# Retention attention in f32 products without halves, inside an attention and two-MoE kernel

## The chip, the cores and the metric

The kernel runs on one core of one Trainium2 chip. The metric is the time of one execution on the device in microseconds; the time of a kernel is the median of its runs. A core has five engines that this text names as the profile does: PE multiplies matrices (PEld is its loading of weights), DVE is the vector engine, ACT the scalar engine, POOL is GpSimd, SP issues most of the transfers. Sixteen DMA engines carry the transfers.

## What is computed

The input is q, k, v of 8 sequences, 8 heads, 576 positions and 64 dimensions. First comes a retention attention (scores with a decay in place of a softmax), then two mixture-of-experts layers on 4608 rows of 512, in which each row goes to one of 8 experts:

```python
scores = scale * np.matmul(q, k.transpose(0, 1, 3, 2))
gamma = 1.0 - 2.0 ** (-5.0 - np.arange(H, dtype=np.float32))
Dmat = np.where(rel >= 0, gamma[:, None, None] ** rel[None, :, :], 0.0)   # rel = i - j
ret = scores * Dmat[None, :, :, :]
return np.matmul(ret, v).astype(np.float32)
...
x = _moe_ref(x=x, **moe_kwargs)        # argmax expert, relu(x @ w1) @ w2, two gates
return _moe2_ref(x=x, **moe2_kwargs)   # the same with a bias by modality and one gate
```

The change touches the attention alone. The routing needs the attention to nearly f32 accuracy, since an argmax that falls otherwise sends a row to another expert.

## The kernel before

The program has two parts. `attention_and_routing` makes the attention output of each tile, its logits and its expert, and scatters the rows into the DRAM buffer `xs1`, sorted by expert. `experts` then runs the two layers from `xs1`; the change does not touch it.

The attention works on 36 chunks of 128 positions and all 8 heads: four per sequence (c = 0 to 3), and one for the last 64 positions of two sequences together (c = 4, the tail). A decay splits into a factor of the key's position, put on v (`v_scale`), and one of the query's position, put on the output (`out`), so the scores only need the causal mask. What earlier chunks of a sequence give comes through a state of 64 by 64 per head, which `kv` and `state` carry from chunk to chunk (`gC` is the decay over one chunk).

PE takes f16 here, so each f32 operand is held as two halves, hi and lo (`k_hi` and `k_lo`, `q_hi` and `q_lo`, `v_hi` and `v_lo`, `a_hi` and `a_lo`, `state_hi` and `state_lo`), and a product is three products, `PASSES = ((0, 0), (0, 1), (1, 0))`. ACT makes the hi halves, DVE and POOL the lo halves. Per chunk:

- three loads of 256 KB on SP's queue (L298): k and v by position, q already transposed in DRAM;
- `transposes` (L329): 8 PE transposes of the halves of k into PSUM, which ACT copies out (`kT_out`);
- `scores` (L350): 24 products, by pairs of heads; the two heads of a pair stand in partitions 0 to 63 and 64 to 127, use the two row halves of the array and write the tiles pa0 and pa1;
- heads of parity 0: DVE masks pa0 into f32 (`a_full`, L420), and `av_full` multiplies with v in f32, four products, the only f32 products of the attention; the trace records each as two matmuls and two weight loads;
- heads of parity 1: hi half by ACT, lo half by DVE (L279), both masked on POOL (L369), and 12 products in `av` (L404);
- `kv` (L377): 24 products and two that add the old state through an identity (L379); `state` (L383);
- `qS` (L404): 24 products of q with the state, in two calls;
- `out` (L431) on DVE, a row scale by `squares` and `row_scale` (L435 to L446), the two halves of the row (`x_hi` on ACT, `x_lo` on DVE, L453), a transposing DMA on SP's queue (L455), and 8 products for the logits (L462).

Groups of 4 or 5 chunks are routed by a chain of about 20 short DVE operations (`route`, L207 to L268), and POOL scatters their rows (L203). The eight first weight pieces of each matrix of expert 0 are converted at the end of this part (L547, L548).

Every engine works in program order. The order is a table, `PLAN`: each step has a beat (one beat is one chunk), given apart for the five kinds of chunk; all steps are sorted by beat. `FIRST` shifts the steps of the first five chunks, `GATES` places the loads and splits of the gate weights, `STEPS` the routing chain.

Of the kernel before, what the change touches and what calls it, by code (L numbers as in the profile page):

```python
# [30 lines left out]
QS, KS, VS = 32.0, 32.0, 16.0  # L31
# [4 lines left out]
    "k_hi": (-2.028, -2.770, -3.081, -2.909, -2.763),  # L36
    "vs": (-1.992, -2.348, -3.188, -1.669, -1.282),
    "k_lo": (-1.751, -2.064, -2.527, -2.579, -2.639),
    "q_hi": (-1.097, -1.702, -1.683, -2.485, -2.161),
    "pt": (-1.401, -1.677, -1.460, -1.290, -1.005),  # L40
    "v_hi": (-0.811, -1.371, -1.336, -0.862, -0.420),
    "q_lo": (-0.551, -1.252, -1.482, -1.253, -0.584),
    "v_lo": (-0.297, -1.046, -0.245, -0.372, 0.196),
    "kT": (-1.159, -0.874, -0.403, -0.701, -0.998),
    "S": (0.222, 0.181, 0.287, 0.260, 0.097),
    "am0": (0.334, 0.282, 0.531, 0.449, 0.187),
    "kv": (0.073, 0.524, 0.372, 0.505, 1.633),
    "Sn": (0.230, 0.575, 0.613, 0.695, 6.213),
    "ah1": (0.596, 0.631, 0.385, 0.518, 0.232),
    "qS0": (-13.770, 0.710, 0.694, 0.529, 0.219),  # L50
    "al1": (0.852, 0.937, 0.839, 0.769, 1.026),
    "Sh": (0.415, 0.944, 0.728, 0.797, -3.479),
    "av0": (0.922, 1.020, 1.097, 1.130, 1.208),
    "Sl": (0.564, 1.233, 0.996, 1.074, -2.260),
    "mh1": (1.231, 1.362, 1.017, 0.873, 1.420),
    "ml1": (1.412, 1.539, 1.052, 1.300, 1.605),
    "av1": (2.106, 1.795, 1.790, 1.802, 2.282),
    "qS1": (-8.214, 2.045, 1.567, 1.937, 1.514),
    "out": (2.400, 2.098, 1.999, 2.210, 2.465),
    "sq": (2.541, 2.150, 3.296, 2.949, 2.775),  # L60
    "rs1": (2.976, 2.479, 3.923, 3.559, 3.293),
    "rs2": (3.315, 3.092, 4.149, 3.806, 3.517),
    "xh": (3.754, 4.304, 4.598, 4.028, 3.781),
    "xl": (4.514, 5.247, 5.077, 4.665, 4.345),
    "lg": (6.437, 7.280, 6.703, 5.707, 5.721),
}
ENGINES = {"vs": "PPPPPPPPP", "v_lo": "PPPPPPPPP", "Sl": "PPPPPPPPP", "mh1": "PPPPPPPPP", "ml1": "PPPPPPPPD"}
FIRST = -3.462, -0.341, 0.344, 0.159, -0.039
GATES = -5.2, -1.440, -2.415, 1.091
WARM = 15  # L70
# [40 lines left out]
def attention_and_routing(tc, st, I, K):  # L111
# [173 lines left out]
    class Chunk:  # L285
# [54 lines left out]
        def q_lo(self):  # L340
            lo(self.qT[:, 1], self.qn, self.qT[:, 0], QS)
# [1141 lines left out]
```

## Time and profile before

| | us |
|---|---|
| median of 3 runs | 1131.69 (1131.39 to 1137.43) |
| the profiled execution | 1131.96 |
| its span, first to last instruction | 1130.2 |
| start until the first scores product | 12.3 |
| first scores product of chunk 0 to that of chunk 35 | 232.0 |
| from there to the first product of the experts | 44.3 |
| experts | 841.6 |

The page gives, over the whole span, PE busy 1025.8 us (91%), DVE 579.8 (51%), ACT 439.8 (39%), POOL 338.2 (30%), and a mean granted TensorE clock of 0.924. The experts hold three quarters of the span, so these shares tell little of the attention; it has to be read by itself. In the attention the row of the granted clock changes between 0.5 and 1.0, which are 1.2 and 2.4 GHz.

### The profile page before, as it was taken

Reading aid. Unit: us, or ns where it says so; the run is one execution under the profiler, and the core shown is the slowest. Engines: PE = TensorE matmul, PEld = TensorE weight load, DVE = VectorE, ACT = ScalarE, POOL = GpSimd, SP = SyncE. Lnnn points to the kernel's source line nnn. Section 1 sums busy time; section 2 is a strip of 40 time slices with the busy share of each in tenths; the row PEclk is TensorE's granted clock in tenths of the full one; section 3 lists DMA queues with packets and bytes.
Section 4 is the critical chain, followed back from the end, with each engine's and each line's share of the span. In section 5 each row is a group of like instructions: output and inputs, shape, how many; then the busy total and the mean of one; then the engine's idle time right before and its main releaser. Section 6 shows DMA issues by size and latency. Waiting matters only on the chain. (4 is left out here: it accounts for less than half of the span.)

```text
span 1130.2 us, 27289 instructions
## 1 busy us (share of the span) xinstructions
PE 1025.8 (91%) x10037; PEld 736.6 (65%) x10037; DVE 579.8 (51%) x1624; ACT 439.8 (39%) x833; POOL 338.2 (30%) x370
## 2 busy tenths in 40 slices
PE   8897788880799999999999999999999999999996
PEld 6786677770566767576666566667676667667664
DVE  7799999986455555555555565532412111111111
ACT  7767666743243434343434434323311111111111
POOL 7868788755112121212211121220110111011010
PEclk8858787865899999999999999999999999999999
DMA  8557677764666566657467455627211121221200
GB/s 297 136 146 188 189 199 199 176 198 126 228 187 149 143 147 151 139 141 144 141 174 172 78 159 128 150 61 208 67 48 45 48 67 40 54 50 47 56 28 31
DMA packets 213056, 145.07 MB, mean 128 GB/s; under 512 B 174089, under 2 KB 174253, under 8 KB 212912
## 3 DMA queue, kind: packets, MB, share of 16 engines
q1 hardware_dynamic: 203952, 114.63, 41.6%
q0 software_dynamic: 8960, 28.62, 7.2%
q8 instruction: 79, 1.29, 0.5%
q14 instruction: 65, 0.53, 0.2%
HBM read 70.75 MB, written 33.92 MB: 93 GB/s over the span
## 5 line engine op out<-in xcount | busy, mean ns | idle before, releaser
L1062 PE MATMUL ph<-xT,wb 128*128 128x256 f16 (+2 forms) x1344 | 338.7, 263 | 22.5 <-PEq L566 22.5
L1064 PE MATMUL ph<-xT,wb 128*128 128x256 f16 (+2 forms) x1344 | 338.8, 263 | 0.0
L1063 PE MATMUL ph<-xT,wb 128*128 128x256 f16 (+2 forms) x1344 | 338.7, 263 | 0.0
L1270 DVE SCALAR_TENSOR_TENSOR hT<-ph,hT 128x512 f16<-128x512 f32 (+2 forms) x168 | 106.5, 638 | 333.3 <-DVEq L566 332.4
L1070 PE MATMUL py<-wb,hT 128*128 128x512 f16 x608 | 231.0, 380 | 1.4 <-PEq L566 0.7
L1071 PE MATMUL py<-wb,hT 128*128 128x512 f16 x608 | 231.1, 380 | 0.0
L1072 PE MATMUL py<-wb,hT 128*128 128x512 f16 x608 | 230.9, 380 | 0.0
L1161 ACT ACTIVATE hT<-ph 128x512 f16<-128x512 f32 (+2 forms) x168 | 93.0, 553 | 225.4 <-ACTq L566 225.3
L1062 PEld LDWEIGHTS ph<-xT,wb 128*128 128x128 f16 x1344 | 131.6, 98 | 40.3 <-issue 23.3
L1063 PEld LDWEIGHTS ph<-xT,wb 128*128 128x128 f16 x1344 | 131.6, 98 | 16.9
L1064 PEld LDWEIGHTS ph<-xT,wb 128*128 128x128 f16 x1344 | 131.6, 98 | 12.9
L1388 POOL DMA_INDIRECT out_dram<-yo,idxo x37 | 35.9, 972 | 333.4 <-POOLq L566 330.1
L1377 POOL TENSOR_SCALAR idx<-v_pos 128x1 int32<-128x1 f32 x39 | 15.5, 397 | 337.7 <-POOLq L566 337.7
L1072 PEld LDWEIGHTS py<-wb,hT 128*128 128x128 f16 x608 | 59.6, 98 | 72.3 <-issue 0.8
L1070 PEld LDWEIGHTS py<-wb,hT 128*128 128x128 f16 x608 | 59.5, 98 | 67.4 <-issue 2.5
L1071 PEld LDWEIGHTS py<-wb,hT 128*128 128x128 f16 x608 | 59.5, 98 | 65.2 <-issue 0.6
L1155 ACT ACTIVATE yo<-py,v_gcol 128x512 f32<-128x512 f32 x37 | 25.4, 687 | 169.0 <-ACTq L566 169.0
L578 DVE SCALAR_TENSOR_TENSOR wb<-stg,wb 128x2048 f16<-128x2048 f32 x36 | 82.5, 2291 | 11.0 <-DVEq L566 11.0
L1138 ACT ACTIVATE wb<-stg 128x2048 f16<-128x2048 f32 x36 | 68.5, 1901 | 0.0
L1149 ACT ACTIVATE sq<-py 128x512 bf16<-128x512 f32 x39 | 23.3, 597 | 113.9 <-ACTq L566 113.9
L1381 POOL DMA_INDIRECT xs<-x2row,idx x39 | 50.3, 1290 | 37.5 <-POOLq L566 37.5
L350 PE MATMUL pa<-qT,kT 64*128 64x128 f16 x864 | 43.9, 260 | 18.1 <-DVE al L279 17.7
(175 smaller groups left out, 1439.2 us busy)
## 6 DMA issues: line engine op xcount, KB each, us to landing
stg<-in_moe_w_dram SPq DMA_DIRECT2D x36, 1024.0 KB, 5.7
kn<-in_k_dram SPq DMA_DIRECT2D x36, 256.0 KB, 3.9
qn<-in_q_dram SPq DMA_DIRECT2D x36, 256.0 KB, 4.2
vn<-in_v_dram SPq DMA_DIRECT2D x36, 256.0 KB, 5.0
w0s<-in_moe_w_dram SPq DMA_DIRECT2D x16, 256.0 KB, 4.4
xs<-zero SPq DMA_DIRECT2D x8, 262.0 KB, 2.9
xs<-zero SPq DMA_DIRECT2D x8, 258.0 KB, 2.5
xT<-xs SPq DMA_TRANSPOSE x42, 4.3
```

Source lines behind the costliest of these rows:

```text
L350: nc.tensor.matmul(self.pa[r][:, hp * P:(hp + 1) * P], self.kT[HALF[r], 4 * x + hp, :], self.qT[HALF[r], y, hp, :], start=(n == 0), stop=( ...
L578: r = fn(*a, **kw).then_inc(self.sem, 1)
L1062: pe.matmul(o, w1(P_, 0)[:, c, fs], xT[s][:, c, cs], start=(c == 0), stop=False)
L1063: pe.matmul(o, w1(P_, 0)[:, c, fs], xT[s][:, 4 + c, cs], start=False, stop=False)
L1064: m = pe.matmul(o, w1(P_, 1)[:, c, fs], xT[s][:, c, cs], start=False, stop=(c == 3))
L1070: pe.matmul(py[b], hT[:, 0, f, bs], w2(P_, 0)[:, f, :], start=(f == 0), stop=False)
L1071: pe.matmul(py[b], hT[:, 0, f, bs], w2(P_, 1)[:, f, :], start=False, stop=False)
L1072: m = pe.matmul(py[b], hT[:, 1, f, bs], w2(P_, 0)[:, f, :], start=False, stop=(f == 7))
L1138: ac.activation(wb[P_ % 2][:, 0, 2048 * c:2048 * c + 2048], stg[:, 2048 * c:2048 * c + 2048], AF.Copy, scale=WS).then_inc(T["cv_full"])
L1161: ac.activation(hT[:, 0, 2 * g:2 * g + 2, cs], ph[g][:, :, cs], AF.Relu).then_inc(T["hh_full"])
L1270: stt(hT[:, 1, 2 * g:2 * g + 2, cs], ph[g][:, :, cs], 0.0, hT[:, 0, 2 * g:2 * g + 2, cs], op0=ALU.max, op1=ALU.subtract).then_inc(T["h_full"])
L1381: po.indirect_dma_start(out=xs2, out_offset=bass.IndirectOffsetOnAxis(ap=idx[b], axis=0), in_=x, in_offset=None, bounds_check=E * R - 1, o ...
```

## The change

All attention products become f32. The hi and lo halves, `PASSES`, the PE transposes of k and their copy are gone; k is loaded a second time, transposed in DRAM by the host (`dk`), as q was. `scores` has 8 products per chunk instead of 24, `kv` 8 instead of 26, `av` 4 for each parity (both masked on DVE into f32), `qS` 4 products of a whole pair of heads: the state of a pair is a 128 by 128 tile with the two heads' states on its diagonal and zeros beside them, kept in 7 fixed tiles.

The decays are taken relative to the middle of the sequence (`gv0` to `gv4`, `gx0` to `gx4`), so that a state needs no factor from chunk to chunk: the new state is the product plus the old one, two DVE additions of 64 partitions by 256, or two ACT copies for c = 0. `PLAN` has one number for each step instead of five, loads are issued 4.5 beats ahead instead of 5.5, `FIRST` and `ENGINES` are gone.

```diff
-    "k_hi": (-2.028, -2.770, -3.081, -2.909, -2.763),
...
+    "vs": -1.3, "S": 0.0, "qS": 0.05, "kv": 0.1, "am0": 0.2, "am1": 0.35, "Sb": 0.5, "av0": 0.8, "av1": 0.85, "out": 1.25,
+    "sq": 1.3, "rs1": 1.65, "rs2": 1.75, "xh": 1.8, "xl": 2.25, "lg": 3.6,
...
+        cols[f"gv{c}"] = g[None, :] ** -at[:, None].astype(np.float64)
+        cols[f"gx{c}"] = g[None, :] ** at[:, None].astype(np.float64) / 8.0
...
+    states = [one.tile([P, 4, P], F32, tag=f"Sb{n}", name=f"Sb{n}") for n in range(7)]
+    for x in states:
+        nc.gpsimd.memset(x, 0.0)
...
         def scores(self):
...
-                for n, (x, y) in enumerate(PASSES):
-                    for r in range(2):
-                        nc.tensor.matmul(self.pa[r][:, hp * P:(hp + 1) * P], self.kT[HALF[r], 4 * x + hp, :], self.qT[HALF[r], y, hp, :], start=(n == 0), stop=(n == 2))
+                for r in range(2):
+                    nc.tensor.matmul(self.pa[r][:, hp * P:(hp + 1) * P], self.pairs("dk")[HALF[r], hp, :], self.pairs("q")[HALF[r], hp, :], start=True, stop=True)
...
+            self.pS = ps.tile([P, 512], F32, tag="pS", bufs=2, name=f"pS{self.tag}")
+            for hp in range(4):
+                for r in range(2):
+                    nc.tensor.matmul(self.pS[HALF[r], hp * HD:(hp + 1) * HD], self.heads("k")[:, 2 * hp + r, :], self.vs[:, 2 * hp + r, :],
+                                     start=(hp == 0), stop=(hp == 3))
...
         def state(self):
...
+            for r in range(2):
+                at = lambda x: x[HALF[r], :, r * HD:(r + 1) * HD]
+                new = self.pS[HALF[r], 0:256].rearrange("p (a d) -> p a d", a=4)
+                if self.c:
+                    nc.vector.tensor_tensor(at(self.Sb), new, at(self.before[0].Sb), op=ALU.add)
+                else:
+                    nc.scalar.activation(at(self.Sb), new, AF.Copy)
...
+                self.gather([(m, slice(2 * hp, 2 * hp + 2), self.pairs("q")[:, hp, part(m)], bf.Sb[:, hp]) for m, bf in enumerate(self.before) for hp in range(4)])
...
-        for L in "kqv":
-            add(i - 5.5, x.load, L)
...
+        for L in ("dk", "q", "v", "k"):
+            add(i - 4.5, x.load, L)
```

In the rows below `a` is the masked scores, `pa` the raw ones, `po` the attention output, `pS` the state product, `pl` the logits, `xT` the transposed row, `dkn`, `qn`, `vn`, `kn` the loaded tiles. On PE, where the scores of a chunk begin, before:

```order
L404 MATMUL po_1_975<-Sh_0_835,qT_1_660 128x64
L404 MATMUL po_2_1118<-vs_2_596,a_2_1108 128x64 x4
L350 LDWEIGHTS kT_3_1058
L350 MATMUL pa_3_0_1198<-qT_3_847,kT_3_1058 128x128
L350 LDWEIGHTS kT_3_1058
L350 MATMUL pa_3_1_1199<-qT_3_847,kT_3_1058 128x128
```

and now, from the last logits product that stands ahead of it:

```order
L357 MATMUL pl_442<-wg_94,xT_3_555 128x48
L304 MATMUL po_2_605<-vs_2_514,a_2_0_619 128x64 x4
L304 MATMUL po_2_605<-vs_2_514,a_2_1_628 128x64 x4
L272 MATMUL pa_3_0_672<-qn_3_377,dkn_3_375 128x128
L272 MATMUL pa_3_1_673<-qn_3_377,dkn_3_375 128x128
```

Now the scores of chunk 3 stand directly behind both mask-dependent products of chunk 2; before, only the f32 products of parity 0 stood there, and those of parity 1 came a beat later.

On DVE, one chunk in the middle of a sequence, before (`al`, `kh` and `qT` are lo halves, `zz`, `z` and `se` steps of a routing chain):

```order
L279 TENSOR_TENSOR al_2_1_2562<-pa_2_1_2443,au_2_1_2499 128x512
L242 TENSOR_TENSOR zz_2564<-lg_2268,oh_2272 128x40
L441 TENSOR_SCALAR eb_114<-ss_113 128x1
L453 SCALAR_TENSOR_TENSOR xr_112<-xg_2_2140,sc_110,xr_112 128x512
L244 TENSOR_REDUCE z_2566<-zz_2564 128x5
L431 TENSOR_TENSOR xg_1_2612<-po_1_2378,cst 128x512
L246 TENSOR_REDUCE se_2274<-ex_2270 128x5
L281 SCALAR_TENSOR_TENSOR kh_0_2571<-kn_0_2035,kh_0_2571 128x512
L445 TENSOR_SCALAR sc_115<-eb_114 128x1
L446 TENSOR_SCALAR iv_116<-eb_114 128x1
L252 TENSOR_SCALAR se_2274<-se_2274 128x5
L281 SCALAR_TENSOR_TENSOR qT_4_2403<-qn_4_1877,qT_4_2403 128x512
```

and now (`dl`, `wq`, `m` and `oh` are steps of a routing chain):

```order
L319 TENSOR_TENSOR a_3_0_697<-pa_3_0_672,mc 128x512
L348 SCALAR_TENSOR_TENSOR xr_121<-xg_1_624,sc_119,xr_121 128x512
L326 TENSOR_TENSOR xg_2_702<-po_2_605,cst 128x512
L189 TENSOR_TENSOR dl_654<-lg_653,mx_658 128x32
L319 TENSOR_TENSOR a_3_1_707<-pa_3_1_673,mc 128x512
L192 SCALAR_TENSOR_TENSOR wq_656<-dl_654,cst 128x32
L288 TENSOR_TENSOR Sb_98<-pS_3_687,Sb_104 64x4x64 x2
L194 TENSOR_REDUCE m_660<-wq_656 128x4
L336 TENSOR_SCALAR eb_118<-ss_117 128x1
L340 TENSOR_SCALAR sc_119<-eb_118 128x1
L341 TENSOR_SCALAR iv_120<-eb_118 128x1
L196 TENSOR_TENSOR oh_657<-wq_656,m_660 128x32
```

Between the two masks of a chunk now stand the lo half of the row of the chunk two before and the output of the chunk before; the lo halves of k, q and the scores are gone.

On SP's queue, between two transposing DMAs, before:

```order
L455 DMA_TRANSPOSE xT_3_1304<-xr_102 128x8x128
L298 DMA kn_1_1425<-in_k_dram 128x512
L298 DMA qn_1_1427<-in_q_dram 128x512
L298 DMA vn_1_1429<-in_v_dram 128x512
L455 DMA_TRANSPOSE xT_0_1432<-xr_107 128x8x128
```

and now:

```order
L350 DMA_TRANSPOSE xT_0_622<-xr_121 128x8x128
L254 DMA dkn_2_632<-in_dk_dram 128x512
L254 DMA qn_2_634<-in_q_dram 128x512
L254 DMA vn_2_636<-in_v_dram 128x512
L254 DMA kn_2_638<-in_k_dram 128x512
L350 DMA_TRANSPOSE xT_1_700<-xr_121 128x8x128
```

Each chunk has four loads between two transposing DMAs where it had three.

## Rows read from the trace of the kernel before

**Rows 1.** Busy time by stretch: length, PE, PEld, DVE, ACT, POOL, clock, DMA share, GB/s.

```profile
12.30:244.30 232.00, 195.37 (x3558) 171.73 (x3556) 218.59 (x475) 159.17 (x313) 182.77 (x186) 0.76 0.70 188
244.30:288.50 44.20, 12.33 (x172) 10.81 (x171) 28.92 (x119) 14.69 (x33) 24.26 (x17) 0.50 0.51 139
288.50:1130.20 841.70, 810.39 (x6258) 550.51 (x6258) 325.20 (x1011) 259.30 (x478) 125.01 (x154) 0.99 0.43 109
...
57.00:84.00 27.00, 25.45 (x359) 22.93 (x359) 25.09 (x54) 16.85 (x35) 17.38 (x18) 0.50 0.52 146
...
207.00:221.00 14.00, 11.62 (x261) 10.08 (x259) 13.73 (x31) 12.71 (x25) 11.67 (x12) 0.99 0.84 189
```

**Rows 2.** Instruction groups of DVE, 12 to 244 us: busy, mean ns, idle before.

```profile
L281 DVE SCALAR_TENSOR_TENSOR kh<-kn,kh 128x512 f16<-128x512 f32 x34 | 39.5, 1162 | 0.0
L453 DVE SCALAR_TENSOR_TENSOR xr<-xg,sc,xr 128x512 f16<-128x512 f32 x31 | 35.3, 1138 | 0.0
L281 DVE SCALAR_TENSOR_TENSOR qT<-qn,qT 128x512 f16<-128x512 f32 x34 | 29.6, 871 | 0.0
L279 DVE TENSOR_TENSOR al<-pa,au 128x512 f16<-128x512 f32 x35 | 23.7, 676 | 0.0
L431 DVE TENSOR_TENSOR xg<-po,cst 128x512 f32<-128x512 f32 x34 | 23.1, 680 | 1.7 <-PE po L404 1.2
L420 DVE TENSOR_TENSOR a<-pa,mc 128x512 f32<-128x512 f32 x32 | 21.9, 685 | 9.9 <-PE pa L350 9.9
L383 DVE TENSOR_TENSOR Sn<-pS,cst 128x256 f32<-128x256 f32 x32 | 13.2, 413 | 1.4 <-PE pS L379 0.8 <-PE pS L377 0.4
```

**Rows 3.** What PE waited for, 12 to 244 us: total, times, longest.

```profile
PE pa L350 <- DVE al L279: 17.7, 10, 3.7
```

**Rows 4.** Timeline of PE: start, length, line, operation, records.

```profile
20.07 1.06 PE L404 MATMUL po<-vs,a 128*128 128x64 f32 x8
20.96 0.22 PE L404 MATMUL po<-vh,ah 128*128 128x64 f16 x2
...
214.72 0.57 PE L377 MATMUL pS<-vh,kh 128*64 128x64 f16 x23 [0.40 <-POOL vh L324]
215.22 1.10 PE L404 MATMUL po<-vs,a 128*128 128x64 f32 x8
216.26 0.84 PE L350 MATMUL pa<-qT,kT 64*128 64x128 f16 x24
217.03 0.62 PE L329 MATMUL pt<-id,kh 128*128 128x128 f16 x8
218.61 0.37 PE L462 MATMUL pl<-wg,xT 128*128 128x48 bf16 x8 [0.96 <-DMA xT<-xr]
...
249.54 1.97 PE L404 MATMUL po<-vs,a 128*128 128x64 f32 x8
```

**Rows 5.** Weight loads (PEld) by group, 12 to 244 us.

```profile
L404 PEld LDWEIGHTS po<-vs,a 128*128 128x128 f32 x272 | 42.0, 236 | 1.7 <-DVE a L420 0.3 <-issue 0.2
L404 PEld LDWEIGHTS <-ah 128*128 128x128 f16 x272 | 17.7, 113 | 1.2 <-issue 0.6
```

**Rows 6.** The hardware DMA queue, 4 to 26 us, loads nearly alone: packets, MB, share.

```profile
q1 hardware_dynamic: 4715, 7.79, 98.6%
```

**Rows 7.** Timeline of the start, all engines.

```profile
7.80 0.25 PE L169 MATMUL pm_mod<-id,mf 36*128 36x36 f32 x1 [1.00 <-DVE id L168]
12.28 1.24 PE L350 MATMUL pa<-qT,kT 64*128 64x128 f16 x24
```

**Rows 8.** Timeline of the end of the attention, all engines.

```profile
244.25 1.11 PE L350 MATMUL pa<-qT,kT 64*128 64x128 f16 x24
253.47 0.69 DVE L431 TENSOR_TENSOR xg<-po,cst 128x512 f32<-128x512 f32 x1 [0.39 <-PE po L404]
257.32 0.75 DVE L453 SCALAR_TENSOR_TENSOR xr<-xg,sc,xr 128x512 f16<-128x512 f32 x1
288.56 0.37 PE L1062 MATMUL ph<-xT,wb 128*128 128x256 f16 x1 [22.52 <-PEq L566]
```

More of the change, by code (lines that the diff above doesn't have):

```diff
@@ L30 @@
 TOK0 = 8192.0
-QS, KS, VS = 32.0, 32.0, 16.0
 WS = 64.0
@@ L290, in __init__ @@
             self.tag = f"{b}_{c}"
-            self.sfx = "t" if self.tail else ""
             self.row = tile_index(b, c)
-            self.src, self.pa, self.au, self.al, self.aa, self.po = {}, {}, {}, {}, ({}, {}), None
-        def load(self, which="kvq"):
-            for L in which:
-                self.src[L] = three.tile([P, 512], F32, tag=f"{L}n", name=f"{L}n{self.tag}", bufs=6)
-                nc.sync.dma_start(self.src[L], I[L][self.row])
-        def on(self, part):
-            turns = ENGINES[part]
-            return nc.vector if turns[self.row % 9] == "D" else nc.gpsimd
+            self.src, self.pa, self.aa, self.po = {}, {}, {}, None
@@ L305, in heads, with load @@
+        def load(self, L):
+            self.src[L] = three.tile([P, 512], F32, tag=f"{L[0]}n", name=f"{L}n{self.tag}", bufs=6)
+            nc.sync.dma_start(self.src[L], I[L][self.row])
         def heads(self, L):
             return self.src[L].rearrange("p (h d) -> p h d", h=H)
-        def k_hi(self):
-            self.kh = two.tile([P, 2, 8, HD], F16, bufs=5, tag="kh", name=f"kh{self.tag}")
-            hi(self.kh[:, 0], self.heads("k"), KS)
-        def k_lo(self):
-            lo(self.kh[:, 1], self.heads("k"), self.kh[:, 0], KS)
@@ L326, in transposes @@
-        def transposes(self):
-            self.pt = ps.tile([P, 8, P], F16, tag="pt", name=f"pt{self.tag}")
-            for i in range(8):
-                nc.tensor.transpose(self.pt[:, i, :], self.kh[:, i // 4, 2 * (i % 4):2 * (i % 4) + 2, :], id16)
-        def kT_out(self):
-            self.kT = two.tile([P, 8, P], F16, bufs=3, tag="kT", name=f"kT{self.tag}")
-            hi(self.kT, self.pt)
-        def q_hi(self):
-            self.qT = two.tile([P, 2, 4, P], F16, bufs=5, tag="qT", name=f"qT{self.tag}")
-            self.qn = self.src["q"].rearrange("p (h i) -> p h i", h=4)
-            hi(self.qT[:, 0], self.qn, QS)
@@ L371, in kv @@
-        def kv(self):
-            self.pS = ps.tile([P, 512], F32, tag="pS", name=f"pS{self.tag}")
-            for h in range(H):
-                hp, r = h // 2, HALF[h % 2]
-                for n, (x, y) in enumerate(PASSES):
-                    nc.tensor.matmul(self.pS[r, hp * HD:(hp + 1) * HD], self.kh[:, x, h, :], self.vh[:, y, h, :], start=(hp == 0 and n == 0), stop=(self.c == 0 and hp == 3 and n == 2))
-            for x in range(2 if self.c else 0):
-                nc.tensor.matmul(self.pS[:, 0:256], id16, self.before[0].Sh[:, x], start=False, stop=(x == 1))
@@ L505, in attention_and_routing @@
             add(last + SCATTER[0] + n * SCATTER[1], scatter, x)
[L507 removed]
+    fetch, convert = first_weights(nc, I, K, lambda n: three.tile([P, 512], F32, tag="dqvk"[n % 4] + "n", bufs=6, name=f"w0s{n}"))
     for n, when in enumerate(WEIGHTS):
```

126 lines of the change are left out of this document (20 added, 106 removed).

## The prediction

> **What bounds the kernel now.** I read the stretches first, since the shares of the page mix attention and experts. From the first scores product to that of chunk 35 pass 232.0 us, 35 chunks of 6.63 us; the change lives there, and the 841.7 us of the experts stay [rows 1]. In those 232 us DVE is busy for 218.6 us, 6.25 us of each chunk, and no other engine is that full: PE has 195.4, POOL 182.8, ACT 159.2, the DMA engines a share of 0.70 [rows 1]. The wait list says the same: the longest wait of PE is that of the scores for the lo half of the scores before, 17.7 us in 10 waits [rows 3], and DVE itself hardly idles ahead of its large groups [rows 2]. So the bound is DVE, and much of what it does is the making of halves. Second, the granted clock of the stretch has a mean of 0.76: it stands at 1.0 or 0.5, so PE spends about 48% of the attention at 1.2 GHz [rows 1]. That costs little while DVE is the bound, but it decides what a heavier load on PE costs.
>
> **The change on DVE.** It loses the lo halves of k, q and the scores and the scaled state, 39.5 + 29.6 + 23.7 + 13.2 = 106.0 us [rows 2]. It gains the second mask, 35 x 0.685 = 24.0 us, by the first mask's row, and for 24 states two additions each. These have half the partitions of the old state's step and the same 256 elements per partition, so I take its 0.413 us for each: 48 x 0.413 = 19.8 us, with 0.2 us each as the lower bound if partitions counted [rows 2]. 218.6 - 106.0 + 43.8 = 156.4 us, or 4.5 us a chunk. DVE is no longer the bound. ACT loses six of its eight large steps and POOL four of six; neither can bind.
>
> **The change on PE.** It loses 8 transposes, 24 + 26 + 24 + 12 f16 products and keeps the 8 logits products; it gains f32 products. The trace has one shape of these: four products of 128 weight columns and 64 moving columns start at 20.07, and the next group starts at 20.96, 0.89 us later, 0.223 us each [rows 4]. At 1.2 GHz the same eight records take 1.97 us instead of 1.10 [rows 1, 4]. For the other shapes I go by the nearest rows:
>
> Scores: 8 products of 64 rows, 128 weight columns and 128 moving columns. In f16, 24 such products take 0.84 us, about 0.2 of it the last one's latency, 0.027 each, while 8 full-height transposes of 128 columns take 0.62, 0.053 each: the two row halves ran beside one another [rows 4]. If f32 does so too and a product costs 0.223 whatever its moving columns, the scores cost 4 x 0.223 = 0.89 us; without the overlap 1.79.
>
> State products: 8 with 64 weight columns, which overlap by column halves now (24 in 0.57 us, 0.016 each [rows 4]). 0.45 us if cost follows the weight columns, 0.89 if not.
>
> q with the state: 4 full products, 0.89 us. Masked scores with v: 8 products, 1.79 us, as measured. Logits: 8 in 0.37, 0.2 without the last latency [rows 4]. The sum is 0.89 + 0.45 + 0.89 + 1.79 + 0.2 = 4.2 us. A change of shape costs something as well: the same f32 group took 1.04 us, not 0.89, until the row-split scores started behind it (215.22 to 216.26) [rows 4]. Four such changes a chunk add 0.6: 4.8 us at 2.4 GHz, 5.3 with the dearer state products, and at 1.2 GHz 2 x 4.2 + 0.6 = 9.0.
>
> The value of 0.223 is what most hangs on. In the row the weight load of an f32 record takes 236 ns on average, that of an f16 one 113 [rows 5], twice as long, and 0.223 us for two records is 0.112 a record. The Trainium skill, page TensorE: Matmul & The Clock Gate, section on weight-path perf modes, says that fast weight load does not apply to f32. By that rule the weight load sets the price, and 128 moving columns cost no more than 64; the row agrees as far as it goes. The Trainium skill, page FP8 and Floating Point Precision, section TensorE Precision Notes, says that true f32 takes four passes through the array. That speaks against a change that puts one f32 product in the place of three f16 ones. By that rule alone the masked-scores products, at 64 columns, would cost half of what the row shows; there the measurement decides, and for 128 columns the two rules meet at the same price.
>
> **The change in the transfers.** Each chunk has a fourth load of 256 KB. In 22 us with almost only loads the hardware queue moved 7.79 MB at a share of 98.6%, so 0.262 MB take 0.73 us of all engines [rows 6]. The stretch now spends 0.70 x 232.0 / 35 = 4.64 us a chunk [rows 1]; 4.64 + 0.73 = 5.4 us. I take the DMA engines as the new floor at 5.4 and 4.9 as the other bound, if packets are shorter when fewer masks and copies use the memory beside them. Loads stand 4.5 beats ahead, some 24 us, so they hide as long as the floor holds; what stands behind them on SP's queue is the transposing DMA, and the logits on PE wait for that.
>
> **The loop between PE and DVE.** The scores of the next chunk stand behind both products with masks, so one turn is scores 0.89 + 0.2 latency, mask, lo half of a row, output, mask on DVE (0.685 + 0.74 to 1.14 + 0.68 + 0.685 [rows 2, 8]), then the last four products with a shape change, 0.89 + 0.2 + 0.15. That is 5.1 to 5.5 us. The additions of the state and most of the routing chain lie in the shadow of PE. PE's own 4.8 us lie within it.
>
> So PE, DMA and the loop all come to 5.0 to 5.5; I take 5.4 for a chunk at 2.4 GHz. At 1.2 GHz PE binds with 9.0. How much of the attention that will be, no row gives. For little of it: PE idles now for 36.6 of 232 us with the work of f16 products, and would idle about 0.6 of 5.4. Against none: in the stretch from 57 to 84 the clock stood at 0.50 although PE was busy for 25.45 of 27.0 us [rows 1]. I take a sixth of the time: 1 / (5/6 / 5.4 + 1/6 / 9.0) = 5.8 us a chunk, 203 us for 35. That is 29.0 us less than now.
>
> **Start and end.** The first scores now stand right behind the transpose of the modality words, which started at 7.80 [rows 7]; they need no halves. The gate loads now stand ahead of the first loads on SP, so I take 8.3 instead of 12.3: 4 us. At the end the output of chunk 35 comes 9.2 us after its scores and the lo half of the last row 3.9 us after that [rows 8]. Now the way from the scores to the output would be 1.1 + 1.4 + 1.3 = 3.8 us, about 5.5 with PE at the lower clock, which saves 3.7. The routing chain and the scatters behind it are the same, but four conversions of weights now stand within the last chain, at 39.36 to 39.83 beats, where three did: one of about 0.7 us more, so 3 us remain.
>
> **The sum.** The profiled execution took 1131.96 us, 1130.2 of them span; the median of the runs is 1131.69, so they stand for one another. 1131.96 - 29.0 - 4 - 3 = 1096 us. At 4.9 us a chunk with the clock always up it would be 1064.
>
> **Rivals.** First, the clock stays down for as much as now, 48%: 1 / (0.52 / 5.4 + 0.48 / 9.0) = 6.7 us a chunk, 2 us more over the stretch, 7 less at its ends: 1127. For it speaks the stretch from 57 to 84; against it that PE waits less.
>
> Second, f32 products of two halves do not run beside one another: scores 1.79, states 0.89, so 5.5 + 0.6 and up to 7.0 with dear state products, say 6.5 us a chunk: 1132 - 4.5 - 7 = 1120, and 1106 to 1138 over its bounds. Against it stands only the f16 row.
>
> Third, and slower: a product is paid by its moving columns, so that 128 cost 2 x 0.223. The tile that four f32 products filled had 64 columns; nothing in the trace shows 128. Scores and q with the state then cost 0.89 more each, and with state products at 0.89 a chunk is 7.0 us: 1132 + 13 - 7 = 1138. If the halves also run one after the other, the scores cost 3.57 and a chunk 9.2 us: 1215. It is slower than before from 6.83 us a chunk on, which is 6.63 + 7 / 35.
>
> **How the numbers follow.** The forecast has 0.57, with 1064 to 1110 as its own range; the first rival 0.12, the second 0.17, the third 0.14. The range goes from 1064 to 1140: it leaves out the dear end of the third (0.09) and faster than all three bounds allow (0.06). A measurement of this kernel tells about 0.5% from no change, 5.7 us. Faster by more than that: the forecast, some of the first rival (0.04) and most of the second (0.13), 0.74. Slower: nearly all of the third, 0.12. In between 0.14.
>
> **What would show it.** Records of scores and q products 0.11 us apart support the price, 0.22 apart the third rival; starts of the two halves' records in pairs, or one by one, decide the second. The starts of the scores give the time of a chunk, 5.8 us; the mean clock of the stretch should be above 0.9. A DMA share near 1.0 would say that the transfers bind, a DVE busy for over 90% that the additions or the small steps were under-counted. Logits that wait for transposed rows behind loads would make the prediction wrong in the slow direction.

## The result and the profile after

| | before, us | after, us |
|---|---|---|
| median of the runs | 1131.54 | 1093.75 (1088.86 to 1098.46) |
| the profiled execution, and its span | 1131.96, 1130.2 | 1091.79, 1090.1 |
| start until the first scores product | 12.3 | 7.0 |
| first scores product of chunk 0 to that of chunk 35 | 232.0 | 205.5 |
| from there to the first product of the experts | 44.3 | 40.5 |
| experts | 841.6 | 837.1 |

The ratio of the times is 0.9664, with a 95% interval from 0.9598 to 0.973. The forecast was 1096.0 us. Two thirds of the 40 us come from the stretch between the scores products, the rest from its two ends and from the experts, which the change doesn't touch.

The windows of the kernel after (columns as in [rows 1]): the stretch, the way from there to the experts, and one stretch at the lower clock:

```profile
7.00:212.40 205.40, 181.57 (x2140) 164.72 (x2140) 156.22 (x435) 57.18 (x132) 66.65 (x64) 0.93 1.00 272
212.40:253.00 40.60, 7.35 (x89) 6.09 (x89) 25.38 (x102) 12.85 (x28) 14.47 (x10) 0.59 0.55 130
...
30.70:42.20 11.50, 11.50 (x90) 10.57 (x90) 5.30 (x11) 2.54 (x6) 2.08 (x2) 0.50 0.69 217
```

DVE fell from 218.6 to 156.2 us of the stretch, ACT from 159 to 57, POOL from 183 to 67. PE is now the fullest engine with 181.6 of 205.4 us, the clock has a mean of 0.93 instead of 0.76, and the DMA engines show a share of 1.00. What is left of idle time on PE, 23.8 us, is nearly all in two waits (wait list of PE, 7 to 212 us, to be read beside [rows 3]: total, times, longest):

```profile
PE po L304 <- DVE a L319: 12.4, 17, 1.2
PE pl L357 <- DMA xT<-xr: 10.5, 10, 3.9
```

The first is the last four products with v, which wait for the second mask on DVE; the second is the logits, which wait for the transposed row. The large groups of DVE in the same stretch (to be read beside [rows 2]):

```profile
L319 DVE TENSOR_TENSOR a<-pa,mc 128x512 f32<-128x512 f32 x64 | 43.7, 685 | 42.1 <-PE pa L272 41.8
L348 DVE SCALAR_TENSOR_TENSOR xr<-xg,sc,xr 128x512 f16<-128x512 f32 x33 | 37.0, 1123 | 0.0
L288 DVE TENSOR_TENSOR Sb<-pS,Sb 64x256 f32<-64x256 f32 x48 | 20.0, 417 | 0.9 <-PE pS L279 0.6
```

DVE, which hardly idled before, now idles 42 us ahead of its masks. The timeline of PE, first a chunk in which nothing waits, then a stretch at the lower clock (start, length, line, operation, records; a length holds the latency of the last record, so the price of a group is the distance to the next start):

```profile
47.70 1.98 PE L304 MATMUL po<-vs,a 128*128 128x64 f32 x16
49.61 1.16 PE L272 MATMUL pa<-qn,dkn 64*128 64x128 f32 x16
50.70 1.16 PE L304 MATMUL po<-Sb,qn 128*128 128x128 f32 x8
51.79 0.69 PE L279 MATMUL pS<-vs,kn 128*64 128x64 f32 x16
52.41 0.37 PE L357 MATMUL pl<-wg,xT 128*128 128x48 bf16 x8
52.62 2.25 PE L304 MATMUL po<-vs,a 128*128 128x64 f32 x16
```

```profile
32.74 1.12 PE L279 MATMUL pS<-vs,kn 128*64 128x64 f32 x16
33.79 0.50 PE L357 MATMUL pl<-wg,xT 128*128 128x48 bf16 x8
34.12 3.65 PE L304 MATMUL po<-vs,a 128*128 128x64 f32 x16
37.70 2.08 PE L272 MATMUL pa<-qn,dkn 64*128 64x128 f32 x16
39.71 2.07 PE L304 MATMUL po<-Sb,qn 128*128 128x128 f32 x8
41.72 0.92 PE L279 MATMUL pS<-vs,kn 128*64 128x64 f32 x16
```

At 2.4 GHz scores cost 1.09 us, q with the state 1.09, the state products 0.62, the logits 0.21 and the masked scores with v 1.91 (47.70 to 49.61): 4.92 us, and PE doesn't idle in such a chunk. At 1.2 GHz the same groups cost 2.01, 2.01, 1.05, 0.33 and 3.58: 8.98 us. The first chunk of a sequence has no product with a state and is 1.09 shorter. Over all chunks PE's work at 2.4 GHz comes to some 163 us (35 x 4.92, less 8 x 1.09 and 4 x 0.2 for the tails). The stretch has 205.5. A mean clock of 0.93 means that 14% of it, 29 us, ran at the lower level, where the work takes 8.98 instead of 4.92; that adds some 13 us. The waits add 24. So 200 of 205.5 us are named.

The price of a single record is read in narrower windows. Of the product of q with the state, with 128 moving columns, two that follow one another (each line is the head of a window of its own and counts the records that run in it):

```profile
50.91 0.39 PE L304 MATMUL po<-Sb,qn 128*128 128x128 f32 x2
...
51.03 0.39 PE L304 MATMUL po<-Sb,qn 128*128 128x128 f32 x2
```

The end of the attention (to be read beside [rows 8]):

```profile
212.43 1.16 PE L272 MATMUL pa<-qn,dkn 64*128 64x128 f32 x16
218.75 0.69 DVE L326 TENSOR_TENSOR xg<-po,cst 128x512 f32<-128x512 f32 x1 [0.45 <-PE pl L217]
221.43 0.75 DVE L348 SCALAR_TENSOR_TENSOR xr<-xg,sc,xr 128x512 f16<-128x512 f32 x1 [0.36 <-ACT xr L345]
252.96 0.37 PE L947 MATMUL ph<-xT,wb 128*128 128x256 f16 x1 [19.74 <-PEq L451]
```

The chunks don't all take the same time. The distances between the scores products are 4.3, 4.7, 4.8, then 9.9, 7.0 and 7.0, and after that anything from 4.9 to 8.3. The three long ones begin with one wait:

```profile
22.08 1.35 SPq L350 DMA_TRANSPOSE xT<-xr  x1
...
27.63 0.37 PE L357 MATMUL pl<-wg,xT 128*128 128x48 bf16 x8 [3.92 <-DMA xT<-xr]
```

The first transposed rows are issued behind the loads of the first seven chunks and land over 5 us later; PE stands for 3.9 us, and from 28.6 to 42.3 the granted clock is at the lower level. The clock falls three more times in this stretch, near 76, 107 and 155 us, and each time a wait of PE ends just before (1.5, 1.2 and 0.7 us long); not every wait is followed by a fall (one of 0.8 us that ended at 142.9 wasn't). What sets the pace after that was the question of the experiments.

### The profile page after: what moved, and what is told of

It reads as the page before. It is cut to its first block, busy times and chain, and to the rows that moved or that the text cites. A ratio compares the mean times of both kernels' runs of the same rounds, so it can differ in the third digit from the quotient of the medians.

```text
span 1090.1 us, 23903 instructions
## 1 busy us (share of the span) xinstructions
PE 1003.2 (92%) x8501; PEld 723.0 (66%) x8501; DVE 508.0 (47%) x1560; ACT 329.5 (30%) x637; POOL 207.9 (19%) x245
## 5 line engine op out<-in xcount | busy, mean ns | idle before, releaser
L304 PE MATMUL po<-vs,a 128*128 128x64 f32 x576 | 80.5, 290 | 12.7 <-DVE a L319 12.4
L304 PEld LDWEIGHTS po<-vs,a 128*128 128x128 f32 x576 | 73.2, 202 | 15.8 <-DVE a L319 15.5
L1262 POOL TENSOR_SCALAR idx<-v_pos 128x1 int32<-128x1 f32 x39 | 10.5, 270 | 334.5 <-POOLq L451 334.5
L319 DVE TENSOR_TENSOR a<-pa,mc 128x512 f32<-128x512 f32 x64 | 43.7, 685 | 42.1 <-PE pa L272 41.8
```

What stands on the lines that cost most here:

```text
L304: nc.tensor.matmul(o, a, b_, start=m in fresh, stop=ends.get(m) == n)
L319: nc.vector.tensor_tensor(d4, s4, self.causal(), op=ALU.mult)
```

## The experiments

All kernels are the kernel after with one edit, unless it says otherwise, and all are compared with the kernel before. "The stretch" is always the time from the first scores product of chunk 0 to that of chunk 35, in the one profiled execution of each kernel; it was 232.0 before and 205.5 after. How much such a stretch varies can be read from e10 and e11 below: their order is the same up to chunk 30, and that part took 155.7 us in one and 162.7 in the other. So a difference of up to 7 us between two stretches is not read as an effect here. In the texts on record theory A (A' later) is that of the prediction: the transfers set the pace. Its rival is that they don't, and that work passed to and fro between engines does; it became theory C on the way.

### Was DVE the bound before?

e7 is the kernel *before*, without the lo halves of k and q on DVE: the products read tiles of zeros instead, so PE does as much as it did.

```diff
-            lo(self.kh[:, 1], self.heads("k"), self.kh[:, 0], KS)
+            pass
...
-            lo(self.qT[:, 1], self.qn, self.qT[:, 0], QS)
+            pass
```

> The kernel before with the DVE steps that make the lo halves of k and q left out; all products stay, with tiles of zeros in the place of these halves, so that the output is less exact and PE, ACT, POOL and the transfers work as before. Theory: DVE is the bound before, so the stretch from the first to the last scores (232.0 us) falls by 25 to 50 us of the 69 us of DVE work removed, to where PE at its mixed clock, DVE and POOL come together. Rival: PE at the lower clock is the bound before, and the stretch falls by less than 10 us.

It took 1106.8 us (one run), and the stretch 201.9 instead of 232.0. Its window:

```profile
10.20:212.00 201.80, 167.91 (x3556) 148.23 (x3552) 164.28 (x409) 158.46 (x315) 165.38 (x188) 0.89 0.86 220
```

DVE was the bound: 54 us less on it (218.6 to 164.3), with every product in place, take 30 us off the stretch, within the 25 to 50 expected. The change itself took off about as much, 26.5 us. So the gain doesn't need cheaper products; that the halves are needless is enough for it.

How much of the 30 us DVE gave directly stays open. PE's idle time is nearly the same in both kernels (36.6 and 33.9 us); what fell is its busy time, from 195.4 to 167.9 us for the same products, since the mean clock is 0.89 instead of 0.76. Whether the clock stayed up because DVE no longer held PE back, or because some operands are zeros now, this run doesn't tell. Before, DVE alone was full where the clock was up (13.7 of 14.0 us); in the long stretch at the lower clock PE was as full as DVE (25.5 and 25.1 of 27.0 us) [rows 1].

### Do the transfers set the pace now?

e1 adds a fifth load of 256 KB per chunk into a tile that nothing reads. e2 leaves one out: k by position isn't loaded, and the state products read the transposed k in its place.

```diff
+            nc.sync.dma_start(again, I["k"][self.row])
```

```diff
-                    nc.tensor.matmul(self.pS[HALF[r], hp * HD:(hp + 1) * HD], self.heads("k")[:, 2 * hp + r, :], self.vs[:, 2 * hp + r, :],
+                    nc.tensor.matmul(self.pS[HALF[r], hp * HD:(hp + 1) * HD], self.heads("dk")[:, 2 * hp + r, :], self.vs[:, 2 * hp + r, :],
...
-        for L in ("dk", "q", "v", "k"):
+        for L in ("dk", "q", "v"):
```

> The changed kernel with a fifth load of 256 KB for each chunk, into a tile that nothing reads. Theory A: in the attention of the changed kernel the transfers set the pace (DMA share 1.00 there), so 36 more loads of 0.73 us make the stretch from the first scores to those of chunk 35 (205.5 us in the changed kernel) 20 to 26 us longer, and the kernel about 1115 to 1120. Rival B: the turn between PE and DVE sets the pace, the full DMA share is only a queue that is kept filled ahead of need, and the stretch grows by less than 5 us.

> The changed kernel with three loads for each chunk: the load of k by position is left out and the state products read the transposed tile in its place, so that output and routing differ and only the stretch up to the last scores counts. Theory A: a chunk falls from 5.87 us to the 5.0 to 5.3 that PE and the loop with DVE need, the stretch from 205.5 to between 175 and 186 us, with a DMA share below 0.97. Rival B: the stretch stays within 5 us of 205.5.

e1 took 1101.3 us, a ratio of 0.9731 (0.9665 to 0.9797), and its stretch 211.0, 5.5 us more. e2 took 1079.9 us (one run; its output and so its routing are others, so only the stretch counts), its stretch 194.3, 11.2 us less. The windows, of e1 and then of e2:

```profile
7.00:218.00 211.00, 181.87 (x2142) 165.08 (x2142) 153.36 (x437) 57.49 (x132) 66.73 (x64) 0.91 1.09 310
```

```profile
6.90:201.20 194.30, 176.53 (x2142) 159.51 (x2142) 158.70 (x439) 57.89 (x132) 66.94 (x64) 0.96 0.93 240
```

A quarter more loads cost 0.16 us a chunk (0.36 if all 7 us by which stretches vary are added), not the 0.73 that they need by [rows 6]. The transfers moved 310 GB/s where they had moved 272, and the share went to 1.09: a share of 1.00 was not the end of them. And the price lies at one place: in e1 the fourth distance is 14.9 us instead of 9.9; in e2 the first six distances lie between 4.3 and 5.2 and sum to 28.8 us instead of 37.7, which is 9 of the 11.2 us. The other 29 distances take 171.5 us in e1, 165.5 in e2 and 167.7 in the kernel after, which is no difference by the measure above. The transfers cost the start, not the steady pace. Theory A, which had 20 to 26 us for e1 and 20 to 30 for e2, falls; rival B, with less than 5 either way, holds for the steady chunks and has nothing on the start.

### Does PE set it?

e3 orders the scores by halves of the array instead of by pairs, so that the two halves run beside one another for a part of the time only.

```diff
-            for hp in range(4):
-                for r in range(2):
+            for r in range(2):
+                for hp in range(4):
```

> The changed kernel with the eight scores products of a chunk ordered by halves, so that no product of the upper rows can run beside one of the lower rows. The two halves overlap now (records of a pair start 7 ns apart), so PE has 0.9 us more per chunk. Theory A: with 4.8 + 0.9 = 5.7 us PE comes up to the floor of the transfers; the stretch grows by 0 to 15 us. Rival B: the turn between PE and DVE is the bound and takes the 0.9 us in full, up to 32 us more.

It took 1100.9 us, a ratio of 0.9733 (0.9672 to 0.9795), with a stretch of 203.1. The scores in its timeline with the first mask, and its waits:

```profile
83.72 1.71 PE L272 MATMUL pa<-qn,dkn 64*128 64x128 f32 x16
...
84.91 0.69 DVE L319 TENSOR_TENSOR a<-pa,mc 128x512 f32<-128x512 f32 x1 [1.26 <-PE pa L272]
...
85.36 1.16 PE L304 MATMUL po<-Sb,qn 128*128 128x128 f32 x8
```

```profile
PE pl L357 <- DMA xT<-xr: 6.5, 8, 1.2
PE po L304 <- DVE a L319: 3.4, 8, 0.9
```

Scores now cost 1.64 us (83.72 to 85.36) instead of 1.09. That is 0.55 more, where 0.9 was expected, and 19 us over 35 chunks. The stretch didn't grow: the waits are 13 us less, and the mean clock of the stretch is 0.97. The first mask needs one half of the scores only and starts 1.19 us after the first product (83.72 to 84.91), as it does in most chunks of the kernel after. So the turn from PE to DVE is no longer than it was, and in the chunks with a wait PE's added work took the place of the wait. In the chunks without one PE does set the pace: there the distance is 5.5 us, where it was 4.9. The two come to little, 170.6 us for the last 29 distances against 167.7; the first six take 32.6 instead of 37.7. Since this order doesn't lengthen the turn, the 32 us of rival B were not put to the test. The time is longer than that of the kernel after because the experts took 845.5 us in the profiled execution. In the same rows the pairs show: ordered by pairs, eight products of two halves cost 1.09 us; sixteen records one after the other, 0.11 apart, would take 1.8.

### Two turns that cover one another

What is left are the two waits. Each belongs to a turn. In the first, scores go to DVE, which makes the first mask, then the lo half and the output of earlier rows, then the second mask, for which PE's last products wait; the next scores stand behind these. In the second, the lo half goes by a transposing transfer to the logits, which stand on PE ahead of the same last products. e4 moves the logits by one beat (the routing chain, which is placed behind them, moves along), e8 the lo half behind the second mask, e9 does both.

```diff
-    "sq": 1.3, "rs1": 1.65, "rs2": 1.75, "xh": 1.8, "xl": 2.25, "lg": 3.6,
+    "sq": 1.3, "rs1": 1.65, "rs2": 1.75, "xh": 1.8, "xl": 2.25, "lg": 4.6,
```

```diff
-    "sq": 1.3, "rs1": 1.65, "rs2": 1.75, "xh": 1.8, "xl": 2.25, "lg": 3.6,
+    "sq": 1.3, "rs1": 1.65, "rs2": 1.75, "xh": 1.8, "xl": 2.40, "lg": 3.6,
```

> The changed kernel with one number altered: the logits of a row stand one beat later in the order (4.6 instead of 3.6 beats), so a transposed row that lies behind the prefetched loads has one chunk more to arrive. Theory C (a steady chunk is set by the turn from PE to DVE and back, 4.9 to 5.0 us, and transfers bind only where the first transposed rows stand behind the loads of seven chunks): the waits of the logits for the transposed row, 10.5 us in the kernel after, fall below 5, the first long intervals (9.9, 7.0 and 7.0 us) shrink, and the stretch of 205.5 us loses 5 to 10 us; the time is 1084 to 1090. Theory A' (the transfers set the pace throughout, the logits only show it): the wait moves to another reader of the queue and the stretch stays within 3 us.

> The changed kernel with one number altered: the lo half of a row (beat 2.40 instead of 2.25) stands behind the second mask on DVE instead of ahead of it, so it is out of the turn that the last products and the next scores wait for. Theory C: a steady turn is shorter by the 0.74 us of the step, and by the 2 us that it takes beside POOL's scatters; since PE needs 4.8 us a chunk itself, the steady chunks fall only from 4.9 or 5.0 to 4.8, but the intervals of 6 to 8 us shrink; the stretch loses 8 to 20 us, the waits of the attention products for the second mask (12.4 us) fall by half or more. The waits for transposed rows may grow by some us, since the rows are split later. Theory A' (transfers): no change within 3 us.

> Both of the two edits: the lo half of a row behind the second mask, and the logits a beat later. Theory C: the two gains lie at different places, so they add up: the stretch of 205.5 us loses 13 to 28 us, to 178 to 192. Theory A': within 3 us of the kernel after.

| kernel | median, us | ratio to before (95%) | stretch, us | its first six distances | the other 29 |
|---|---|---|---|---|---|
| after | 1093.75 | 0.9664 (0.9598 to 0.973) | 205.5 | 37.7 | 167.7 |
| e4, logits later | 1088.9 | 0.9588 (0.9547 to 0.963) | 195.5 | 28.5 | 167.1 |
| e8, lo half later | 1095.9 | 0.9692 (0.9638 to 0.9747) | 208.0 | 33.8 | 174.2 |
| e9, both | 1076.9 | 0.9477 (0.9424 to 0.953) | 184.8 | 31.1 | 153.7 |

The two waits of PE over the whole stretch, in e4, e8 and e9:

```profile
PE po L304 <- DVE a L319: 12.0, 12, 1.7
...
PE pl L357 <- DMA xT<-xr: 1.0, 1, 1.0
```

```profile
PE pl L357 <- DMA xT<-xr: 23.9, 19, 4.4
...
PE po L304 <- DVE a L319: 1.0, 2, 0.8
```

```profile
PE po L304 <- DVE a L319: 4.6, 10, 1.1
PE pl L357 <- DMA xT<-xr: 3.4, 3, 2.3
```

e8 shows it best. The wait for the mask is gone, as theory C said, and the time did not move, which it did not say: the wait for the transposed row took all of it, 23.9 instead of 10.5 us. The 8 to 20 us expected of it are missed. The lo half and the logits stand 1.20 beats apart in e8, and one such pair in its timeline is this:

```profile
93.14 1.23 SPq L350 DMA_TRANSPOSE xT<-xr  x1
...
100.47 0.50 PE L357 MATMUL pl<-wg,xT 128*128 128x48 bf16 x8 [3.12 <-DMA xT<-xr]
```

The row is issued at 93.14 and is there at 100.47, 7.3 us later; 1.2 beats of 4.9 us are 5.9. Where the transfer takes longer than that, the turn sets the pace. With one beat more (e9) it seldom does, and with the other wait mostly gone too the stretch falls by 20.7 us, where the two edits alone gave 9.9 and nothing. e4 and e9 came out within their numbers (9.9 us of 5 to 10, 184.8 of 178 to 192). But e4's gain lies all in the first six distances, the stall at the start; over the other 29 neither edit alone gives anything, and both together give 14.0 us. The kernels below that have both edits (e10, e11 and e12) take 152 to 157 us for these 29, those with one edit or none 165 to 174 (e14, with the rows on another queue, apart). So the steady pace of the kernel after was set by both turns, now one, now the other; each hid the other.

### What is left, and the fetch of the first weights

e10 goes on from e9: output, squares and row scales 0.2 beats later as well, out of the first turn, and the fetch of the first expert's weights behind the last loads. e11 is the same with the fetch where it was.

```diff
-    "vs": -1.3, "S": 0.0, "qS": 0.05, "kv": 0.1, "am0": 0.2, "am1": 0.35, "Sb": 0.5, "av0": 0.8, "av1": 0.85, "out": 1.25,
-    "sq": 1.3, "rs1": 1.65, "rs2": 1.75, "xh": 1.8, "xl": 2.25, "lg": 3.6,
+    "vs": -1.3, "S": 0.0, "qS": 0.05, "kv": 0.1, "am0": 0.2, "am1": 0.35, "Sb": 0.5, "av0": 0.8, "av1": 0.85, "out": 1.45,
+    "sq": 1.5, "rs1": 1.85, "rs2": 1.95, "xh": 2.0, "xl": 2.40, "lg": 4.6,
...
-        add(NT - 5.7 + n / 3, fetch, n)
+        add(NT + 0.5 + n / 100, fetch, n)
```

> The changed kernel with the steps of a row moved behind the masks of the next chunk: output at 1.45 beats instead of 1.25, squares and row scales 0.2 later, lo half at 2.40, logits at 4.6; and the fetch of the first expert's weights goes behind the loads of the last chunk. The turn on the path is then scores, first mask, second mask, last four products: 0.9 + 0.2 + 0.7 + 0.7 + 1.2 us, under PE's own 4.8. Theory C: PE becomes the bound, chunks of 4.8 to 5.0 us at 2.4 GHz, a stretch of 172 to 185 us and a time of 1060 to 1075. Against it stands the transfers' share: if it holds the pace at 5.4 us a chunk after all, the stretch stays above 190 us. The tail may grow by up to 3 us, since the last weights arrive later.

> The steps of a row behind the masks of the next chunk, as in the kernel before this one in the study (output at 1.45 beats, squares and row scales 0.2 later, lo half at 2.40, logits at 4.6), but with the fetch of the first expert's weights where the changed kernel has it. Theory C: the stretch stays at 181 us within 4, since the late fetch did nothing for the pace, and the end of the attention is again 38 to 41 us, not some 48; the time is 1068 to 1076. Theory A' (the fetch beside the last chunks took the transfers from them): the stretch grows by over 5 us.

e10 took 1086.3 us (0.9566, 0.9524 to 0.9607), although its stretch is the shortest, 181.0 us. The time went to the end:

```profile
199.28 11.99 SPq L428 DMA_DIRECT2D w0s<-in_moe_w_dram  x16
212.87 1.25 SPq L350 DMA_TRANSPOSE xT<-xr  x1
...
218.34 0.50 PE L357 MATMUL pl<-wg,xT 128*128 128x48 bf16 x8 [16.69 <-DMA xT<-xr]
```

From the last scores product at 188.0 to the experts at 242.1 it takes 54.1 us, 14 more than after: the last transposed row stands behind the sixteen weights in the queue. The expectation had put 3 us on that. With the fetch where it was (e11) the end is 38.4 us again and the time 1072.7 (0.9484, 0.9411 to 0.9557). Its stretch, 188.2, is 7 us longer than that of e10, the number of A' and not of C. But the fetch is not the reason: the first weight is issued at 172.0 us in e11, and the 7 us lie before that, in the first 30 distances (162.7 us against 155.7), where both kernels do the same; the last five take 25.6 and 25.3. What differs is the clock, whose mean over the stretch is 0.93 in e11 and 0.97 in e10; PE idles 12.0 us of it in both. Moving the output as well gave nothing that can be told from e9.

### POOL beside DVE

The lo half takes 0.74 us at some places and over 2 at others, in before and after. In the kernel after, the slow ones stand beside POOL's work (timeline of DVE and POOL, three places):

```profile
17.81 0.74 DVE L348 SCALAR_TENSOR_TENSOR xr<-xg,sc,xr 128x512 f16<-128x512 f32 x1
18.02 1.44 POOL L264 TENSOR_TENSOR vs<-vn,cst 128x512 f32<-128x512 f32 x1 [3.21 <-DMA vn<-in_v_dram]
...
97.23 2.27 DVE L348 SCALAR_TENSOR_TENSOR xr<-xg,sc,xr 128x512 f16<-128x512 f32 x1
97.90 1.05 POOL L264 TENSOR_TENSOR vs<-vn,cst 128x512 f32<-128x512 f32 x1
...
186.43 1.04 POOL L264 TENSOR_TENSOR vs<-vn,cst 128x512 f32<-128x512 f32 x1 [4.56 <-DMA vn<-in_v_dram]
186.51 1.50 DVE L348 SCALAR_TENSOR_TENSOR xr<-xg,sc,xr 128x512 f16<-128x512 f32 x1
```

At 186.51 DVE's step ends 0.54 us after POOL's step on v; at 97.23 too it ends 0.55 us after, though it began first by the records. At 17.81 DVE's step keeps its 0.74 us, and POOL's takes 1.44 instead of 1.04.

e13 is the kernel after with the factors on v made by ACT; e12 is e11 with the same edit.

```diff
-            nc.gpsimd.tensor_tensor(self.vs, self.heads("v"), col(f"gv{self.c}").unsqueeze(2).to_broadcast([P, 8, HD]), op=ALU.mult)
+            g = col(f"gv{self.c}")
+            for h in range(8):
+                nc.scalar.activation(self.vs[:, h, :], self.heads("v")[:, h, :], AF.Identity, scale=g[:, h:h + 1])
```

> The changed kernel with nothing else altered but that the factors on v are made by ACT instead of POOL. If POOL's work stretches the lo half (mean 1.12 us in the kernel after, 0.74 where nothing stands beside it), its mean falls under 0.95; since the lo half stands in the turn from PE to DVE there, the stretch of 205.5 us loses 4 to 10 us, less what the waits for transposed rows take back. If the transfers stretch it, the mean stays above 1.05 and the stretch within 3 us.

> The kernel of e11 with the factors on v made by ACT, eight steps of 64 columns each, instead of one POOL step of 1.04 us. If it is POOL's work beside DVE that stretches DVE's steps from SBUF to SBUF (lo half 0.74 us alone, 1.6 to 2.5 beside POOL), the mean of the lo half falls from about 1.1 to under 0.95, since then only the scatters stand beside it, and the stretch loses 2 to 6 us. If the stretching has another cause (the transfers into SBUF, which stay), the mean stays above 1.05 and the stretch within 2 us. ACT takes some 1.6 to 2.4 us a chunk more and idles enough for it.

The lo half in e13, then two of its waits:

```profile
L350 DVE SCALAR_TENSOR_TENSOR xr<-xg,sc,xr 128x512 f16<-128x512 f32 x33 | 24.5, 743 | 3.3 <-ACT xr L347 3.3
```

```profile
PE pl L359 <- DMA xT<-xr: 16.0, 12, 3.3
PE po L306 <- DVE a L321: 5.1, 8, 0.8
```

The mean falls from 1123 to 743 ns, so it was POOL's step on v that stretched it; the scatters, which are still there and which e8's expectation had named, don't. The masks, the output and the additions, which take one operand from PSUM, have the same mean in both kernels (685 and 686, 680 and 682, 417 and 418 ns). And the time? 1090.6 us (0.9651, 0.9601 to 0.97), with a stretch of 205.3: no change, as in e8 and for the same reason. The wait for the mask fell by 7.3 us and that for the rows rose by 5.5. e12, where both turns are out of the way, took 1070.8 us (0.9467, 0.9425 to 0.9509) with a stretch of 185.0; from e9 and e11 it can't be told apart. The 4 to 10 us expected of e13 are missed; e12's stretch is 3.2 us under e11's, within the 2 to 6 expected, but two executions of one order differ by more, so that bears nothing out. What makes the step slow was right, and in e13 the step lay on no path that ended last.

### A queue of its own for the transposed rows

Does a row land late because it stands behind loads in SP's queue? e14 is e8 with the transposing transfers issued on ACT's queue.

```diff
-            nc.sync.dma_start_transpose(self.xT, self.xr)
+            nc.scalar.dma_start_transpose(self.xT, self.xr)
```

> The kernel of e8 (lo half behind the second mask, logits as in the changed kernel), with the transposing transfers issued on ACT's queue instead of SP's, where all loads stand. In e8 the logits waited 22.1 us for transposed rows, and the stretch was 208.0 us. If a transposed row is late because it stands behind prefetched loads in one queue, its own queue takes it past them: the waits fall under 6 us, the stretch to 185 to 195 us and the time to 1072 to 1083. If the transfers as a whole are too slow (their share of 1.0 is a limit), it arrives as late as before and the stretch stays within 4 us of 208. ACT now waits for the lo half before it issues; where that holds up copies of states, the waits for them would grow by 5 us or more and take some of the gain.

It took 1148.7 us, a ratio to before of 1.0157 (1.0079 to 1.0235), and its stretch is 256.5 us, 48.5 more than that of e8. Its wait for the rows, and its two hardware queues from 40 to 200 us (packets, MB, share of 16 engines):

```profile
PE pl L357 <- DMA xT<-xr: 40.2, 18, 5.3
...
q1 hardware_dynamic: 12467, 22.69, 48.9%
q10 hardware_dynamic: 23232, 5.77, 28.9%
```

Both theories are wrong here: the rows came later, not earlier and not as before. Two things can be read off. In 160 us, 22 transposing transfers (5.77 MB by 0.262) took 46.2 us of all engines, 2.1 us each; 87 loads took 78.2 us, 0.9 each. So a transposed row costs the transfers somewhat more than two loads. And the loads changed too: SP, which in e8 waited for lo halves ahead of each transposing transfer and held the loads back by that, now issues them as soon as a buffer is free (its loads wait 95.8 us for scores products that free one, 4.4 us in e8), so that more of them run beside the rows. Which of these makes the rows later isn't settled by this run. Nor are the waits most of the 48.5 us: PE idles 41.0 us of the stretch where it idled 26.2 in e8, and its busy time grew from 181.7 to 215.5 us with the same products, since the mean clock fell from 0.91 to 0.77.

## Why the prediction was right, point by point

**DVE was the bound, and is not any more.** Right, by e7, with the clock's part in its 30 us left open. The sum was 156.4 us for the stretch, and 156.2 were measured; the additions of the state took 0.417 us each where 0.413 was assumed, so the pieces of 64 partitions cost as much as those of 128.

**The price of an f32 product.** Right. The records of the state product with q, with 128 moving columns, stand 0.11 us apart (50.91 to 51.03), as those of the masked scores with 64 do; the records of the scores come in pairs, one of each half, 7 ns apart, and the pairs again 0.11 apart. That refutes the second and the third rival. (The third rival's dear end of 9.2 us a chunk doesn't follow from its own terms, which give 8.8, or 9.7 if the state products don't overlap either; the forecast doesn't use it.) The Trainium skill, page FP8 and Floating Point Precision, section TensorE Precision Notes, has f32 take four passes; by that alone 64 columns would cost half of 128, and the rows show no such difference (0.11 us a record for both). The shapes came out at 4.92 us a chunk, where the sum was 4.8, and at 8.98 at the lower clock, where it was 9.0; the terms of the attention products were each 0.1 to 0.2 too low (scores 1.09, not 0.89), and the 0.6 for changes of shape made up for it.

**The clock.** A sixth of the time was assumed at the lower level; the mean of 0.93 says 14%. Right in size, which leaves the first rival's 48% out, though it was a guess: the runs don't show what brings the clock down, only that each of the four falls came behind a wait of PE.

**The transfers as the floor.** Wrong. This is the step that failed: 4.64 + 0.73 = 5.4 us was taken from a share of the DMA engines, as if the share times the length were work that can't be squeezed. e1 moved a quarter more in nearly the same time, and in e9 many chunks follow one another at 4.9 us with all four loads. Nor does any run show the shorter packets of the lower bound: a load took 0.9 us of all engines in e14, not less than the 0.73 of [rows 6]. The sentence that a share near 1.0 "would say that the transfers bind" is wrong too: the share came out at 1.00, and they didn't.

**What took its place.** At 2.4 GHz a chunk needs 4.65 us of PE on average (163 / 35), and the waits add 24 / 35 = 0.68: 5.3 us, near the 5.4 of the forecast, by another way. Half of these waits is the turn between PE and DVE, which the prediction had as 5.1 to 5.5 us; it had the turn right (the chunk from 49.61 to 54.81 takes 5.2), and e9 shows that it counts only together with the second. The other half, the logits behind the transposed rows, the prediction named as what would make it wrong, without a price. The price was 10.5 us, and 23.9 as soon as the first turn was out of the way. By the prediction's own formula PE's 4.8 us alone give a stretch of 182 us, 23 too short, and the turn alone, at 5.3, gives 199. So the forecast had one right reason and one wrong one for the same 5.4, and that it came within 3 us is in part luck: the wrong floor covered the wait for the rows, which had no term.

**Start, end, experts.** The start gave 5.3 us (4 forecast), the end 3.8 (3). The experts took 4.5 us less, which nothing forecast; over the kernels here, which all have the same experts, they take from 836.7 to 847.0, so this is no effect of the change. With 841.6 us again the profiled execution would have taken 1096.

## What to carry to other kernels

Splitting f32 into f16 halves was paid here on the vector engine more than on PE: look which engine makes the halves, and whether it is the one that binds, before comparing the products. Where two waits of an engine are of like size, take both away in one run before judging either: alone, e8 and e13 showed nothing, e4 showed 9.9 us at the start of the stretch and nothing behind it, and two edits together 20.7. Before a stretch of one execution is read, it helps to know how much two executions of the same order differ: 7 us here. And a busy share of the transfers near 1.0 was no bound here; a load that nobody reads tells in one run whether there is room.

## What was not expected of the hardware

A DVE step that reads two operands from SBUF takes 0.74 us alone and up to 2.3 us beside POOL's multiplication on SBUF tiles, while steps of the same size that take one operand from PSUM keep their 0.68; with that multiplication on ACT the mean is 0.743 and the scatters on POOL don't matter (e13). The Trainium skill, page SBUF — State Buffer, section SBUF: two separate sides, says that DVE and GpSimd share a pair of ports as an exclusive lock, which a DVE operation with two SBUF inputs takes against a GpSimd operation that reads SBUF; the trace agrees: in all 14 places of the kernel after where the DVE step is slow, it ends 0.54 to 0.56 us after POOL's, and in the one place where it isn't slow beside that step, POOL's is (17.81). In six of the 14 DVE's step began 0.2 to 0.7 us before POOL's by the records, each time with a scatter running on POOL; why it waits there all the same, the runs don't show.

The DMA engines' share of a stretch went from 1.00 to 1.09 and 1.11 while the rate rose from 272 to 310 GB/s (e1) and 296 (e9). And a transposing transfer took 2.1 us of all engines where a load of the same 256 KB took 0.9 (e14).
